# Pooling batch 0's v on VectorE from a second load, and adding the band's mask of batches 0 and 1 on TensorE

## The chip, the cores and the metric

The kernel runs on one core of one Trainium2 chip. The metric is the time of one execution on the device, in microseconds (us). A core has TensorE (PE, matrix products into PSUM), VectorE (DVE), ScalarE (ACT), GpSimd (POOL) and SyncE (SP, which issues the transfers of this kernel); each works through its own queue in order and waits for the others by semaphores. PEld is the load of a matrix into TensorE.

## What is computed

Three layers, each feeding the next, all in float32. Cut to what matters:

```python
# q, k, v: (4 batches, 8 heads, 576 rows, 64); factor 4
q_d, k_d, v_d = mean over groups of 4 rows of q, k, v          # 144 rows
out_d  = softmax(q_d @ k_d.T / 8) @ v_d                         # pooled attention
mask   = abs(i - j) < 4
out_l  = softmax(where(mask, q @ k.T / 8, -1e9)) @ v            # band attention, 7 wide
x      = repeat(out_d, 4 rows) + out_l                          # (2304, 512)
x      = (sigmoid(x @ w_gate) * (x @ w_val)) @ w_out            # layer 1, 1536 wide
h      = x @ w_in;  out = (h * sigmoid(1.702 * h)) @ w_out2     # layer 2, 2048 wide
```

## The kernel before

**Order.** The program is written as operations (`op`, line 112), each with an engine, a length in ns, the buffers that it reads and writes, and a due time. `Plan.order` (line 143) runs a list scheduler once, ahead of the launch: at each step it takes the engine that is free first and, of what is ready on it, the operation with the earliest due time; a transfer counts 230 bytes a ns and 2.2 us. The result is one fixed order for each engine. `BEGIN` (line 95) says when each engine is free of the work that stands ahead of the plan. In that plan, wherever TensorE would idle, matmuls of a constant tile `warm` into a spare PSUM bank are put in (L1420), at least one ahead of each small matmul operation until the second layer-1 product begins. `port=True` marks VectorE operations that in the plan don't overlap GpSimd's.

**Attention.** A `Job` is one batch and one pair of heads; there are four jobs to a batch, 0 to 3 being batch 0. In `pools`, GpSimd sums groups of four columns of q and k (L636, L638). `scores` computes the band in 24 tiles of 24 query rows by 30 keys into a PSUM pair of banks (L668), VectorE adds the mask while it copies the scores into `sc` (L684), takes the maximum (L694), subtracts it (L695), ScalarE takes the exponential (L697), VectorE sums, divides and transposes (L698 to L702). There is one buffer `sc`, so that a job's scores wait until the exponential of the job before has read it. The pooled scores (L710) get their softmax by L727 to L750. `down_t` transposes the pooled weights (L770, L775), `values` multiplies them by the pooled v, `vd` (L807), `band` multiplies the band's weights by v (L785), and L820 combines both. Three pairs of banks serve batch 0, one serves the other batches. Jobs 5 and later are "merged": their pooled scores share the pair of the band's scores.

**v.** `Values` holds 256 columns of v of one batch (two jobs' worth). `vt` has v in overlapping tiles of 32 rows for the band. For batches 1 to 3, `load` also brings v once more as `vg`, four rows side by side, and `pool` sums them on VectorE (L601, L603). Batch 0 has no `vg`: `pool_tiles` sums the rows of `vt` with a matrix of ones on TensorE (L590, 12 products of 256 columns, two instructions each) and ScalarE copies the result (L594). GpSimd makes the ones in 13 instructions (`make_ones`, L1367 to L1374), queued between the poolings of jobs 0 and 1.

**Layers.** A weight arrives packed in 64 bits; `convert` (L851 to L857) makes it float32 by one ScalarE and three VectorE operations, and `parts_of` (L864, L867) splits it in two parts for three products (L927, L928, L929). Four buffers receive packed weights. Layer 1 of batch 0 uses the converted weights as they come, beside attention of batch 1.

The lines that the change touches most:

```python
op("pe", 2700.0, pe, [ones, vt], [ss, vd], at)                                    # 593
op("act", act_ns(2 * VC, True), lambda: nc.scalar.copy(vd.t, ss.t[:GH, :, :VC]), [ss], [vd], at)
...
op("pool", 1500.0, make_ones, [], [ones], -4.0e3)                                 # 1377
```

Of the kernel before, what the change touches and what calls it, by code (L numbers as in the profile page):

```python
# [19 lines left out]
P = 128  # L20
# [58 lines left out]
class Plan:  # L79
# [14 lines left out]
    WARM_LEAST = 1  # L94
    BEGIN = {"pe": 0.0, "act": 2000.0, "dve": 2200.0, "pool": 3900.0, "sp": 600.0}

# [191 lines left out]
def tile_multiscale_attention_gated_ffn(  # L288
# [11 lines left out]
    D = 64  # L300
# [76 lines left out]
    for nm, n, shape in (("qt", 2, [P, S + 8]), ("kt", 2, [P, KPAD + S + 5]), ("vt", 0, [P, NG, VC]),  # L377
                         ("sc", 1, [P, 2, NG, NU]), ("pt", 2, [P, 2, NG, 32]), ("tt", 2, [P, 2, NG, 32]),
                         ("vg", 1, [GH, 2, 4, VC]), ("half", 1, [P, G, 2]),
                         ("qd", 2, [P, G]), ("kd", 2, [P, G]), ("vd", 2, [GH, 2, VC]),  # L380
                         ("pd", 2, [GH, 2, 2, G]), ("pdt", 1, [GH, 2, 2, G]), ("up", 2, [P, G]), ("ones", 1, [P, 102]),
                         ("xf", 2, [P, S])):
        aslots += ring(nm, n, shape, F32, apool)
# [5 lines left out]
    for n, x in enumerate(wslots[-8:]):  # L389
        x.under = (firsts[n // 2],)  # L390
    small = apool.tile([P, 4, 2, NG], F32, name="small", tag="small")
    smalld = apool.tile([GH, 4, 4], F32, name="smalld", tag="smalld")
# [75 lines left out]
    warm = sb.tile([P, P], BF16, name="warm", tag="warm")  # L468
    nc.vector.memset(warm, 0.0)
    for s in [*qslots, *plan.rings["qt0"][0]]:  # L470
# [36 lines left out]

    def dma(out_, in_, nbytes, reads, writes, due, after=0.0):
        op("sp", nbytes, lambda: nc.sync.dma_start(out=out_, in_=in_), reads, writes, due, after)

# [29 lines left out]
    class Values:  # L540
# [6 lines left out]
        def load(self):  # L547
# [30 lines left out]

        def pool_tiles(self):


            vt, vd = self.vt, self.vd
            at = self.job.due(0.55)
            ss = bank(self.job.banks)

            def pe():
                for g in range(NG):
                    for kh in range(2):
                        ks, o = slice(64 * kh, 64 * kh + 64), 30 - 6 * g
                        nc.tensor.matmul(ss.t[:GH, kh, :VC], ones.t[ks, o:o + GH], vt.t[ks, g],  # L590
                                         start=g == 0, stop=g == NG - 1, tile_position=(64 * kh, 0))

            op("pe", 2700.0, pe, [ones, vt], [ss, vd], at)
            op("act", act_ns(2 * VC, True), lambda: nc.scalar.copy(vd.t, ss.t[:GH, :, :VC]), [ss], [vd], at)  # L594

        def pool(self):
            if not self.b:
                return self.pool_tiles()
            vg, vd = self.vg, self.vd
            at = self.job.due(0.4)  # L600
            op("dve", dve_ns(4 * VC), lambda: nc.vector.tensor_add(  # L601
                vg.t[:, :, :2], vg.t[:, :, :2], vg.t[:, :, 2:]), [], [vg], at, port=True)
            op("dve", dve_ns(2 * VC), lambda: nc.vector.tensor_add(vd.t, vg.t[:, :, 0], vg.t[:, :, 1]),  # L603
               [vg], [vd], at, port=True)

    class Job:
# [49 lines left out]
        def scores(self):  # L656
# [15 lines left out]
            when = self.due(0.1)  # L672
            if not self.merged:
                op("pe", 1500.0, scored, [qt, kt], [ss, sc], when)
            else:
                qd, kd, nmd, smd, pd = self.qd, self.kd, self.nmd, self.smd, self.pd

                def pe():
                    scored()
                    self.pooled(ss, n)  # L680

                op("pe", 1700.0, pe, [qt, kt, qd, kd],
                   [ss, sc, nmd, (smd, 0), (smd, 1), (pd, 0), (pd, 1)], when)
            op("dve", dve_ns(2 * n), lambda: nc.vector.tensor_add(  # L684
                sc.t.rearrange("p h g c -> p h (g c)"), ss.t[:, :, :n],
                mask.rearrange("p g c -> p (g c)")[:, None, :].to_broadcast([P, 2, n])), [ss], [sc], when)
            if self.merged:
                self.pooled_softmax(ss, n, when, [sc])

# [3 lines left out]
            at = self.due(0.15)  # L693
            op("dve", dve_ns(2 * n), lambda: nc.vector.reduce_max(nm.t, sc.t, axis=AX.X), [sc], [nm], at)  # L694
            op("dve", dve_ns(2 * n), lambda: nc.vector.tensor_sub(sc.t, sc.t, spread(nm)), [nm], [sc], at, port=True)  # L695
            p = pt.t[:, :, :, :NU]
# [666 lines left out]

    ones = buf("ones")

    def make_ones():
        nc.gpsimd.memset(ones.t, 0.0)  # L1367
        for i in range(4):
            c = 30 + 36 * (i % 2)
            part = ones.t[32 * i:32 * i + 32, c:c + 6]  # L1370
            nc.gpsimd.memset(part, 1.0)
            nc.gpsimd.affine_select(out=part, in_=part, pattern=[[-4, 6]], compare_op=ALU.is_ge,
                                    fill=0.0, base=-3, channel_multiplier=1)
            nc.gpsimd.affine_select(out=part, in_=part, pattern=[[4, 6]], compare_op=ALU.is_ge,  # L1374
                                    fill=0.0, base=6, channel_multiplier=-1)
# [8 lines left out]
    for n in range(2):  # L1384
        halves[0, n].vt, halves[0, n].vd = buf("vt"), buf("vd")
    halves[0, 0].load()
    back = []
    for n in range(len(jobs) + 1):
# [9 lines left out]
        if n + 2 < len(jobs):  # L1398
            if n + 2 >= NHP:
                jobs[n + 2].load()  # L1400
            if n % 2 == 0:
                halves[divmod(n // 2 + 1, 2)].load()
# [63 lines left out]
```

## Time and profile before

| | |
|---|---|
| median of 3 runs | 923.15 us (922.99 to 925.22) |
| the profiled execution | 925.11 us |
| its span in the trace | 923.4 us |
| TensorE busy | 909.3 us, 98% |
| VectorE busy | 757.0 us, 82% |
| ScalarE busy | 508.3 us, 55% |
| GpSimd busy | 80.8 us, 9% |
| DMA moved | 113.76 MB, mean 123 GB/s |

The span is what the trace covers. All lines of the sections below come from this one execution. Busy shares are means over stages that differ: attention of batch 0 alone (to about 46 us), then layer 1 of batch 0 with attention of batch 1 beside it, and so on, so the stages have to be looked at one by one. A matmul's end is modelled in the trace and overlaps the next one's start.

### The profile page before, as it was taken

How to read it: one execution, taken by the hardware profiler on the slowest of the kernel's cores; microseconds unless marked ns; L12 is line 12 of the kernel's file. 1: busy time of each engine (PE TensorE's matmuls, PEld its weight loads, DVE VectorE, ACT ScalarE, POOL GpSimd, SP SyncE). 2: the span in 40 equal slices, each digit the busy share in tenths (PEclk: the TensorE clock that was granted, in tenths of full speed). 3: DMA queues.
4: the chain of work that ended last, by engine and by line, in shares of the span. 5: the costliest groups of instructions: out<-in, count | busy, mean ns of one | idle time of the engine just before them, and what ended most of it. 6: DMA issues, size and time to landing. Idle time of an engine off the chain costs nothing.

```text
span 923.4 us, 18997 instructions
## 1 busy us (share of the span) xinstructions
PE 909.3 (98%) x7378; PEld 761.8 (83%) x7378; DVE 757.0 (82%) x1432; ACT 508.3 (55%) x1094; POOL 80.8 (9%) x123
## 2 busy tenths in 40 slices
PE   8999999999999999999999999999999999999997
PEld 4677787788888887889999998888888888888896
DVE  4899998988878888899999898878977887765474
ACT  3756664645555555565545655545664553554463
POOL 6211201111011100010000000000301100000000
PEclk8999999999999999999999999999999999999999
DMA  9448548365375834434311651102531100152101
GB/s 287 124 155 229 188 157 244 110 183 174 114 204 185 248 108 135 159 110 141 109 49 42 222 193 46 46 24 84 190 115 69 46 35 34 40 180 78 43 4 23
DMA packets 63949, 113.76 MB, mean 123 GB/s; under 512 B 8241, under 2 KB 29563, under 8 KB 63858
## 3 DMA queue, kind: packets, MB, share of 16 engines
q1 hardware_dynamic: 63858, 112.54, 39.2%
q8 instruction: 58, 0.95, 0.5%
q14 instruction: 33, 0.27, 0.1%
HBM read 82.37 MB, written 30.15 MB: 122 GB/s over the span
## 4 chain that ended last, share of the span: by engine, by line
PE 94%; DVE 2%; POOL 1%; DMA 1%; issue 1%; ACT 1%; POOLq 0%; ACTq 0%
PE ph L927 13%; PE ph L929 13%; PE ph L928 13%; PE acc L927 8%; PE acc L928 8%; PE acc L929 8%; PE pa L927 7%; PE pa L928 7%; PE pa L929 7%; PE pa L785 2%; PE pa L668 1%; PE pa L710 1%; PE pa L770 1%; PE pa L807 1%; PE acc L1420 1%
## 5 line engine op out<-in xcount | busy, mean ns | idle before, releaser
L864 ACT CAST whi<-w 128x512 fp32r<-128x512 f32 x151 | 92.4, 613 | 77.4 <-PE ph L929 28.3
L927 PE MATMUL ph<-xhi,whi 128*128 128x512 f32 (+1 forms) x322 | 127.6, 396 | 0.0
L929 PE MATMUL ph<-xlo,whi 128*128 128x512 f32 (+1 forms) x322 | 124.4, 386 | 0.0
L928 PE MATMUL ph<-xhi,wlo 128*128 128x512 f32 (+1 forms) x322 | 124.4, 386 | 0.0
L867 DVE TENSOR_TENSOR wlo<-w,whi 128x512 fp32r<-128x512 f32 x149 | 103.9, 699 | 17.5 <-ACT whi L864 17.3
L864 ACT CAST whi<-wr 128x512 fp32r<-128x512 f32 (+1 forms) x99 | 55.7, 565 | 35.9 <-PE acc L929 16.5
L867 DVE TENSOR_TENSOR wlo<-wr,whi 128x512 fp32r<-128x512 f32 (+1 forms) x99 | 62.2, 630 | 15.6 <-ACT whi L864 14.7
L927 PE MATMUL acc<-ghi,whi 128*128 128x512 f32 (+1 forms) x192 | 73.7, 384 | 0.0
L927 PEld LDWEIGHTS ph<-xhi,whi 128*128 128x128 f32 x322 | 60.9, 189 | 14.7 <-issue 1.6
L1041 DVE TENSOR_TENSOR w<-pa,w 128x512 f32<-128x512 f32 (+1 forms) x112 | 70.2, 627 | 3.3 <-PE pa L929 2.6
L928 PE MATMUL acc<-ghi,wlo 128*128 128x512 f32 (+1 forms) x192 | 72.4, 377 | 0.4 <-DVE wlo L867 0.4
L929 PE MATMUL acc<-glo,whi 128*128 128x512 f32 (+1 forms) x192 | 72.3, 377 | 0.5 <-DVE glo L867 0.5
L929 PEld LDWEIGHTS ph<-xlo,whi 128*128 128x128 f32 x322 | 60.8, 189 | 12.5
L928 PEld LDWEIGHTS ph<-xhi,wlo 128*128 128x128 f32 x322 | 61.0, 189 | 11.3
L927 PE MATMUL pa<-w,whi 128*128 128x512 f32 (+1 forms) x168 | 61.5, 366 | 0.1
L929 PE MATMUL pa<-w,whi 128*128 128x512 f32 (+1 forms) x168 | 61.4, 366 | 0.0
L928 PE MATMUL pa<-w,wlo 128*128 128x512 f32 (+1 forms) x168 | 61.4, 366 | 0.0
L864 ACT CAST w<-w 128x512 fp32r<-128x512 f32 x51 | 31.1, 619 | 35.7 <-PE pa L929 20.4
L867 DVE TENSOR_TENSOR w<-w,w 128x512 fp32r<-128x512 f32 x48 | 34.3, 721 | 17.0 <-ACT w L864 16.8
L961 ACT ACTIVATE th<-ph 128x512 f32<-128x512 f32 (+1 forms) x44 | 24.6, 559 | 42.8 <-PE ph L929 42.8
L927 PEld LDWEIGHTS acc<-ghi,whi 128*128 128x128 f32 x192 | 36.0, 188 | 7.4 <-issue 1.7
L966 DVE SCALAR_TENSOR_TENSOR th<-th,ph 128x512 f32<-128x512 f32 (+1 forms) x44 | 27.9, 634 | 17.1 <-PE ph L929 12.2
(286 smaller groups left out, 2307.0 us busy)
## 6 DMA issues: line engine op xcount, KB each, us to landing
w<-w SPq DMA_DIRECT2D x68, 512.0 KB
w2d<-we SPq DMA_DIRECT2D x32, 256.0 KB
w<-gd SPq DMA_DIRECT2D x32, 256.0 KB
gd<-w SPq DMA_DIRECT2D x30, 256.0 KB
st<-x2d SPq DMA_DIRECT2D x52, 128.0 KB
w<-w2d SPq DMA_DIRECT2D x16, 256.0 KB
wr<-w2d SPq DMA_DIRECT2D x16, 256.0 KB
out<-ev SPq DMA_DIRECT2D x16, 256.0 KB
```

Source lines behind the costliest of these rows:

```text
L668: nc.tensor.matmul(ss.t[32 * i:32 * i + 32, h, g * NU:(g + 1) * NU], qt.t[hs, NQ * t:NQ * t + 32], kt.t[hs, NQ * t:NQ * t + NU], start=Tru ...
L710: nc.tensor.matmul(ss.t[:GH, h, c + r * G:c + (r + 1) * G], qd.t[h * D:(h + 1) * D, r * GH:(r + 1) * GH], kd.t[h * D:(h + 1) * D, :], star ...
L770: nc.tensor.transpose(ss.t[:GH, h, o:o + GH], pd.t[:, h, r, kh * GH:(kh + 1) * GH], ident.t[:GH, :GH])
L785: nc.tensor.matmul(ss.t[h * D:(h + 1) * D, s, q:q + NQ], vt.t[ks, g, v0 + h * D:v0 + (h + 1) * D], tt.t[ks, h, g, :NQ], start=True, stop=T ...
L864: op("act", act_ns(n), lambda: nc.scalar.copy(vh(), vm()), [rm], [rh], due)
L867: return lambda: on.tensor_sub(vl(), vm(), vh().bitcast(F32))
L927: nc.tensor.matmul(o, lhi, rhi, start=first, stop=False, skip_group_check=more)
L928: nc.tensor.matmul(o, llo, rhi, start=False, stop=False, skip_group_check=more)
L929: nc.tensor.matmul(o, lhi, rlo, start=False, stop=last, skip_group_check=more)
L961: op("act", act_ns(n, True), lambda h=h: nc.scalar.activation(th.t[:, :n], h.t[:, :n], AF.Tanh, scale=0.5 if layer == 1 else 1.702 / 4.0), ...
L966: op("dve", dve_ns(n), lambda: nc.vector.scalar_tensor_tensor(th.t[:, :n], th.t[:, :n], 1.0, hb[-1].t[:, :n], op0=ALU.add, op1=ALU.mult), ...
L1041: op("dve", dve_ns(N), lambda: nc.vector.tensor_add(tmp.t[:, o, :N], b.t[:, :N], tmp.t[:, i, :N]), [b, (tmp, i)], [(tmp, o)], t)
```

## The change

Half 0 of batch 0's v is loaded a second time into `vg`, half 1 into two new buffers `vg1`, which lie where layer-1 weights 10 and 11 come later. `pool` sums both halves on VectorE; for half 1 the two row blocks are loaded and summed apart. `pool_tiles`, the ones and their products go. For batches 0 and 1 the mask is kept in bf16, and TensorE adds it: a product of the identity (bf16, now the content of `warm`) and the mask opens each accumulation, the scores are added to it, and VectorE's maximum and subtraction read the scores from PSUM. Batches 2 and 3 keep the add on VectorE. The identity is made first on GpSimd, in bf16, and VectorE copies it to float32.

```diff
-    BEGIN = {"pe": 0.0, "act": 2000.0, "dve": 2200.0, "pool": 3900.0, "sp": 600.0}
+    BEGIN = {"pe": 0.0, "act": 2000.0, "dve": 4400.0, "pool": 4300.0, "sp": 600.0}
...
+    seconds = [Slot(x.rearrange("p a b -> p (a b)").bitcast(F32).rearrange("p (r d) -> p r d", r=4)[:GH])
+               for x in top[2:4]]
+    plan.ring("vg1", seconds)
+    for n, x in enumerate(wslots[20:24]):
+        x.under = (seconds[n // 2],)
...
-    nc.vector.memset(warm, 0.0)
+    make_identity(nc, warm)
...
-    mask = sb.tile([P, NG, NU], F32, name="mask", tag="mask")
+    mask = sb.tile([P, 2, NG, NU], BF16, name="mask", tag="mask")[:, 0]
...
+    maskb = mask.rearrange("p g c -> p (g c)")
-    op("pool", 650.0, lambda: make_identity(nc, ident.t), [], [ident], -10.0e3)
+    nc.vector.tensor_copy(ident.t, warm)
...
+                if hp:
+                    self.vg = [buf("vg1") for _ in range(2)]
+                else:
+                    self.vg = buf("vg")
+                for kh in range(2):
+                    x, t = (self.vg[kh], self.vg[kh].t) if hp else ((self.vg, kh), self.vg.t[:, kh])
+                    dma(t, v[b, kh * 4 * GH:(kh + 1) * 4 * GH, c].rearrange("(g r) d -> g r d", r=4),
+                        GH * 4 * VC * 4, [], [x], -16.5e3 if hp else -19.1e3, 13.0e3 if hp else 6.0e3)
...
-        def pool_tiles(self):
...
+            if isinstance(vg, list):
+                for kh, x in enumerate(vg):
+                    op("dve", dve_ns(2 * VC), lambda x=x: nc.vector.tensor_add(x.t[:, :2], x.t[:, :2], x.t[:, 2:]),
+                       [], [x], at, port=True)
+                    op("dve", dve_ns(VC), lambda kh=kh, x=x: nc.vector.tensor_add(vd.t[:, kh], x.t[:, 0], x.t[:, 1]),
+                       [x], [(vd, kh)], at, port=True)
+                return
...
+            masked = self.b < 2
             def scored():
+                for h in range(2 if masked else 0):
+                    nc.tensor.matmul(ss.t[:, h, :n], warm, maskb, start=True, stop=False, skip_group_check=True)
...
-                                         start=True, stop=True, tile_position=(h * D, 32 * i))
+                                         start=not masked, stop=True, tile_position=(h * D, 32 * i),
+                                         skip_group_check=masked)
...
-            op("dve", dve_ns(2 * n), lambda: nc.vector.tensor_add(
+            x = ss if masked else sc
+            if not masked:
+                op("dve", dve_ns(2 * n), lambda: nc.vector.tensor_add(
...
+            def scores_of():
+                return ss.t[:, :, :n].rearrange("p h (g c) -> p h g c", c=NU) if masked else sc.t
+            op("dve", dve_ns(2 * n), lambda: nc.vector.reduce_max(nm.t, scores_of(), axis=AX.X), [x], [nm], at)
+            op("dve", dve_ns(2 * n), lambda: nc.vector.tensor_sub(sc.t, scores_of(), spread(nm)),
+               [nm, x] if masked else [nm], [sc], at, port=not masked)
...
-    op("pool", 1500.0, make_ones, [], [ones], -4.0e3)
...
-    halves[0, 0].load()
+    for n in range(2):
+        halves[0, n].load()
```

## Rows read from the trace of the kernel before

**Rows 1.** The page, part 4: the chain that ended last, by engine.
```profile
PE 94%; DVE 2%; POOL 1%; DMA 1%; issue 1%; ACT 1%; POOLq 0%; ACTq 0%
```
**Rows 2.** Windows (us): busy us (instructions) of PE, PEld, DVE, ACT, POOL; clock; DMA share; GB/s.
```profile
12.00:46.00 34.00, 31.94 (x836) 21.80 (x837) 24.48 (x51) 21.65 (x65) 10.73 (x16) 0.90 0.63 198
46.00:135.00 89.00, 88.28 (x1069) 69.79 (x1068) 86.54 (x158) 56.03 (x130) 12.46 (x13) 1.00 0.62 183
```
**Rows 3.** Timeline of GpSimd: start, length, line, output and input; [idle before and releaser].
```profile
6.93 0.18 POOL L1367 MEMSET ones<- 128x102 f32 x1
...
10.39 0.67 POOL L636 TENSOR_TENSOR half<-qt 128x288 f32<-128x288 f32 x1
...
15.14 0.67 POOL L636 TENSOR_TENSOR half<-w 128x288 f32<-128x288 f32 x1 [2.17 <-DMA w<-qT]
```
**Rows 4.** Timeline of TensorE, 7 to 25 us; neighbours of one kind are merged (x).
```profile
7.94 1.69 PE L1420 MATMUL acc<-warm 128*128 128x512 bf16 x7
13.03 1.24 PE L710 MATMUL pa<-kd,qd 64*72 64x144 f32 x8 [3.41 <-POOL kd L638]
...
14.74 1.22 PE L668 MATMUL acc<-kt,qt 64*32 64x30 f32 x96
...
16.43 4.17 PE L590 MATMUL acc<-vt,ones 64*72 64x256 f32 x24
...
21.57 2.81 PE L590 MATMUL pa<-vt,ones 64*72 64x256 f32 x24
```
**Rows 5.** Window 12 to 19 us, columns as in Rows 2.
```profile
12.00:19.00 7.00, 5.97 (x118) 3.65 (x120) 3.97 (x9) 3.08 (x13) 4.36 (x8) 0.53 1.04 356
```
**Rows 6.** Timeline of ScalarE: the copy of the pooled v, the first weight's conversion.
```profile
20.68 0.58 ACT L594 COPY vd<-acc 72x512 f32<-72x512 f32 x1 [3.79 <-PE acc L590]
...
24.91 0.66 ACT L851 ACTIVATE wr<-w 128x512 f32<-128x512 f32 x1
```
**Rows 7.** Timeline of VectorE: three operations that waited.
```profile
22.53 0.54 DVE L698 TENSOR_REDUCE small<-pt 128x12 f32<-128x372 f32 x1 [4.36 <-ACT pt L697]
...
28.17 0.76 DVE L820 TENSOR_TENSOR xf<-acc,up 128x576 f32<-128x576 f32 x1 [0.68 <-PE acc L785]
...
34.31 0.76 DVE L820 TENSOR_TENSOR xf<-pa,up 128x576 f32<-128x576 f32 x1 [0.69 <-PE pa L785]
```
**Rows 8.** Windows of 7.1 to 46 us, columns as in Rows 2.
```profile
7.10:25.60 18.50, 15.09 (x231) 8.87 (x232) 9.50 (x20) 9.20 (x32) 9.56 (x25) 0.82 0.88 276
25.60:46.00 20.40, 19.37 (x623) 13.98 (x622) 18.64 (x38) 14.59 (x43) 5.09 (x6) 1.00 0.50 136
```
**Rows 9.** Lines L601, L603, L684, L695: count, ns shortest/median/longest, first and last start.
```profile
L601 DVE TENSOR_TENSOR vg<-vg x6: 1209/1214/1216, 63.2 to 306.9; 72x1024 f32<-72x1024 f32 x6
L603 DVE TENSOR_TENSOR vd<-vg x6: 677/680/680, 64.9 to 310.6; 72x512 f32<-72x512 f32 x6
L684 DVE TENSOR_TENSOR sc<-acc,mask x3: 495/524/531, 16.0 to 36.3; 128x360 f32<-128x360 f32 x3
L695 DVE TENSOR_TENSOR sc<-sc,small x16: 518/533/716, 8.8 to 360.0; 128x360 f32<-128x360 f32 x16
```
**Rows 10.** Timeline of SP: one load of vg for batch 1 being issued.
```profile
29.53 0.82 SPq L509 DMA_DIRECT2D vg<-v  x1
```
**Rows 11.** Windows of 1 us, columns as in Rows 2: the DMA share and GB/s are last.
```profile
8.00:9.00 1.00, 1.00 (x7) 0.44 (x6) 1.00 (x3) 0.05 (x1) 0.82 (x4) 1.00 1.09 221
...
21.00:22.00 1.00, 1.00 (x12) 0.65 (x12) 0.00 (x0) 0.80 (x3) 0.00 (x0) 1.00 1.03 393
...
24.00:25.00 1.00, 1.00 (x29) 0.46 (x28) 0.51 (x1) 0.57 (x2) 0.00 (x0) 1.00 0.00 0
...
34.00:35.00 1.00, 1.00 (x68) 0.74 (x67) 0.69 (x2) 0.27 (x2) 0.00 (x0) 1.00 0.84 180
```
**Rows 12.** Timeline of TensorE at 140 us, in layer 1 of batch 0.
```profile
140.20 0.89 PE L785 MATMUL pa<-tt,vt 30*64 30x24 f32 x48 [1.09 <-DVE tt L702]
```
**Rows 13.** Window right behind it, columns as in Rows 2.
```profile
142.00:144.00 2.00, 2.00 (x6) 1.56 (x6) 2.00 (x4) 0.65 (x2) 0.00 (x0) 0.52 0.91 339
```

More of the change, by code (lines that the diff above doesn't have):

```diff
@@ L380, in tile_multiscale_attention_gated_ffn @@
                          ("qd", 2, [P, G]), ("kd", 2, [P, G]), ("vd", 2, [GH, 2, VC]),
-                         ("pd", 2, [GH, 2, 2, G]), ("pdt", 1, [GH, 2, 2, G]), ("up", 2, [P, G]), ("ones", 1, [P, 102]),
+                         ("pd", 2, [GH, 2, 2, G]), ("pdt", 1, [GH, 2, 2, G]), ("up", 2, [P, G]), ("pad", 1, [P, 102]),
                          ("xf", 2, [P, S])):
@@ L506, in pool_ns, with dma @@
         return 140.0 + 2.12 * n
-    def dma(out_, in_, nbytes, reads, writes, due, after=0.0):
-        op("sp", nbytes, lambda: nc.sync.dma_start(out=out_, in_=in_), reads, writes, due, after)
+    def dma(out_, in_, nmaskeds, reads, writes, due, after=0.0):
+        op("sp", nmaskeds, lambda: nc.sync.dma_start(out=out_, in_=in_), reads, writes, due, after)
     QUANTUM = 3 * 227.0
@@ L577, in load @@
                 d, after)
-        def pool_tiles(self):
[L582 to L594, printed above, removed]
         def pool(self):
-            if not self.b:
-                return self.pool_tiles()
             vg, vd = self.vg, self.vd
             at = self.job.due(0.4)
+            if isinstance(vg, list):
[5 more added lines that the diff above has]
+                return
             op("dve", dve_ns(4 * VC), lambda: nc.vector.tensor_add(
@@ L669, in scored @@
                                          qt.t[hs, NQ * t:NQ * t + 32], kt.t[hs, NQ * t:NQ * t + NU],
-                                         start=True, stop=True, tile_position=(h * D, 32 * i))
+                                         start=not masked, stop=True, tile_position=(h * D, 32 * i),
+                                         skip_group_check=masked)
             when = self.due(0.1)
             if not self.merged:
-                op("pe", 1500.0, scored, [qt, kt], [ss, sc], when)
+                op("pe", 1500.0 + 200.0 * masked, scored, [qt, kt], [ss, sc], when)
             else:
@@ L680, in pe @@
                     self.pooled(ss, n)
-                op("pe", 1700.0, pe, [qt, kt, qd, kd],
+                op("pe", 1700.0 + 200.0 * masked, pe, [qt, kt, qd, kd],
                    [ss, sc, nmd, (smd, 0), (smd, 1), (pd, 0), (pd, 1)], when)
-            op("dve", dve_ns(2 * n), lambda: nc.vector.tensor_add(
-                sc.t.rearrange("p h g c -> p h (g c)"), ss.t[:, :, :n],
-                mask.rearrange("p g c -> p (g c)")[:, None, :].to_broadcast([P, 2, n])), [ss], [sc], when)
+            x = ss if masked else sc
+            if not masked:
+                op("dve", dve_ns(2 * n), lambda: nc.vector.tensor_add(
+                    sc.t.rearrange("p h g c -> p h (g c)"), ss.t[:, :, :n],
+                    mask.rearrange("p g c -> p (g c)")[:, None, :].to_broadcast([P, 2, n])), [ss], [sc], when)
             if self.merged:
-                self.pooled_softmax(ss, n, when, [sc])
+                self.pooled_softmax(ss, n, when, [x])
             def spread(x):
@@ L693, in scores @@
             at = self.due(0.15)
-            op("dve", dve_ns(2 * n), lambda: nc.vector.reduce_max(nm.t, sc.t, axis=AX.X), [sc], [nm], at)
-            op("dve", dve_ns(2 * n), lambda: nc.vector.tensor_sub(sc.t, sc.t, spread(nm)), [nm], [sc], at, port=True)
+            def scores_of():
[3 more added lines that the diff above has]
+               [nm, x] if masked else [nm], [sc], at, port=not masked)
             p = pt.t[:, :, :, :NU]
@@ L1362, in tile_multiscale_attention_gated_ffn @@
     seven = [0]
[L1364 to L1375, printed above, removed]
-    op("pool", 1500.0, make_ones, [], [ones], -4.0e3)
     jobs = [Job(b, hp) for b in range(B) for hp in range(NHP)]
@@ L1400, in tile_multiscale_attention_gated_ffn @@
                 jobs[n + 2].load()
-            if n % 2 == 0:
+            if n % 2 == 0 and n:
                 halves[divmod(n // 2 + 1, 2)].load()
```

## The prediction

> **What bounds the kernel now.** I read the page's chain first: TensorE carries 94% of it [rows 1]. That is a mean over stages, so I read the stages next [rows 2]. From 46 to 135 us TensorE is busy 88.28 of 89 us, but VectorE is busy 86.54 of the same 89, since it turns the layer-1 weights into fp32 and splits them there. Both engines are full, and neither can gain alone. From 12 to 46 us, where attention of batch 0 runs, VectorE is busy only 24.48 of 34 us. All that the change touches in batch 0 lies there, so I followed who waits for whom.
>
> Three stalls hang together. (1) GpSimd builds the matrix of ones from 6.93 us on and comes to job 1's pooling of q and k only at 10.39, 3.4 us later but for gaps [rows 3]; TensorE sits idle for 3.41 us until that pooling ends at 13.0 [rows 4]. Job 1's scores, whose data are there, are queued behind the waiting matmul and come at 14.74. [...] (3) The pooling of v by the ones takes 4.17 us there and 2.81 us once the clock is back, 7.0 in all [rows 4]. ScalarE has the copy of its result next in its queue and waits 3.79 us for it; VectorE waits 4.36 us for job 1's exponential, which is behind that copy [rows 6, 7]. So in 7.1 to 25.6 us VectorE is busy 9.50 of 18.50 us: 9.0 us idle. From 25.6 to 46 it is idle 1.76 us [rows 8].
>
> The profiled execution took 925.1 us (span 923.4 and 1.7 around it); the median is 923.15, 2.0 less. I sum against 925.1 and take 2.0 off at the end.
>
> **The change part by part.** *TensorE.* The 7.0 us of pooling go. The ones go from GpSimd, so job 1's q and k can be pooled right after job 0's: end near 7.0 + 2.6 = 9.6 us instead of 13.0 (2.6 is 13.03 less 10.39, the same four operations before). Job 1's scores, behind it in the queue, move as far, to some 11.3. If the idle is gone the clock need not fall; of the 3.4 us of other work at 13.0 to 16.4 about half, 1.5 us, comes back. Together TensorE could stand 3.4 + 7.0 + 1.5 = 12 us earlier. Added are two bf16 matmuls of 180 columns per job in 8 jobs. No row has them. Seven bf16 matmuls of 512 columns take 1.69 us, 0.24 each [rows 4]; scaled by columns 0.085, unscaled 0.24, so 16 cost 1.4 to 3.9 us. They only add work, so no gain is possible. I take 1.4, since columns are what such a matmul streams; half of it lies in batch 0 beside slack, 0.7 in batch 1 on a full TensorE.
>
> *VectorE.* The mask's add, 0.525 us, goes from 8 jobs: 2.1 us in batch 0, 2.1 in batch 1 [rows 9]. Added in batch 0: for half 0 the two adds of batches 1 to 3, 1.214 and 0.68 us; for half 1 two pairs of half that length. By the line through those two rows, 1.04 ns an element, the pair costs 0.68 and 0.41, twice 1.09. Sum 4.07. Net in batch 0: +2.0 us; in batch 1: -2.1.
> The maximum and the subtraction now read PSUM. The add, which reads PSUM, takes 0.524 us and the subtraction, from SBUF, 0.533 [rows 9], so I price that at nothing; ends: -0.02 and +0.02 us each. [...]
> The scores' PSUM pair is held through the maximum and the subtraction, about 1.06 us longer. Batch 0 has three pairs and loses the two holders of the pooling; in batch 1 the merged jobs hold their pair for the exponentials anyway. Nothing, with that cover; without it 1 us a job.
>
> *ScalarE* loses both copies and, what counts, the wait ahead of the first [rows 6].
>
> *DMA and SP.* Four loads of 0.295 MB, in runs of 1 KB, are issued: two ahead of the q and k of jobs 2 and 3, two between those and the first weights. Each issue holds SP about 0.82 us [rows 10], 3.3 in all. The engines are full until about 22 us [rows 11], so the bytes cost more than the issue. No row has this load alone in the same place: v's tiles go at 221 GB/s early on, and the 1 KB runs of batch 1 near 180; q, k and weights at 393 [rows 11]. Hence 1.18 MB take 3.0 to 6.6 us; I take 5.3 (221), the row in the same traffic. The first q of job 2, awaited until 15.1 us [rows 3], lands near 17.8 (two loads, 2.7 us, now stand ahead of it). The weights land about 5.3 us later. Their cover: DMA stands still at 24 to 25 us [rows 11] while the first converted weight is only touched at 24.91 [rows 6]. So the first conversion need not start later than before, but it cannot start earlier either.
> [...]
> In VectorE's queue the adds can wait for these loads, with job 1's softmax behind them; that is in the idle below.
>
> *Small moves.* The identity is now made first on GpSimd, so the warming matmuls begin later by its time, and the scores of job 0 with them; the missing add repays it. VectorE's copy of the identity ends long before the first scores. Nothing.
>
> **The sum.** TensorE gains 12 us but can use only what VectorE feeds it. VectorE has 9.0 us idle before 25.6. I keep 4.0 of it: the wait for the first scores, the exponential of job 0, and the later data of jobs 2 and 3; this is an estimate, with ends 2 (the first two alone) and 7 (the loads bind). Lead at 25.6 us: 9.0 - 4.0 - 2.0 = 3.0. Of the idle after that, two waits of 0.68 and 0.69 us for TensorE's last band product go [rows 7]: 4.4. Batch 1's masks give 2.1 more by 135 us and cost TensorE 0.7; this counts only where VectorE is late, as at 140 us, where TensorE waits 1.09 us for it [rows 12]. I count 0.6 and forecast 5.0 us. Afterwards TensorE is the bound and nothing gives it back. 925.1 - 5.0 = 920.1, less 2.0: **918.1 us**. With the ends of the kept idle, 7 and 0 for batch 1, 2 and all of its 2.1: 1.4 to 8.5 us, 921.7 to 914.6.
>
> **The rivals.** *TensorE is the bound after all.* If weights are early enough, nearly all 12 us arrive, less 0.7: 925.1 - 11.3 - 2.0, about 912. For: TensorE's 94% of the chain. Against: VectorE's 97% in the same stage.
> *The new loads eat it.* At 180 GB/s weights come 6.6 us late, VectorE runs out of attention work before they land, and the kept idle is 7 or more. The lead is then 0 at 25.6 and the rest 0 to 1.4: 921.7 to 923.2, call it 922.5. For: DMA is full until 22 us. Against: the engines stood still at 24 us with weights at hand. That the new order keeps conversions where they were gives the same time.
> *Slower: TensorE starved in the first layer.* With less to do in front, TensorE stands ahead of VectorE and waits for weights from 46 to 140 us. The place at 140 us shows the price of one such wait: 1.09 us, and then 0.52 of full clock for 2 us, which loses 1.0 more [rows 12, 13]: 2.1 a time. A lead of 1.4 is used up by one; three more cost 6.3, with 0.7 for the masks: 923.15 - 1.4 + 6.3 + 0.7 = 928.8. It decides from the second wait on if the lead is small, the fourth if it is 5. For: VectorE has 2.5 us of slack in 89. Against: the change takes 2.1 us from VectorE just there.
>
> **How the numbers follow.** Forecast 0.48 (915 to 920.3 as its own range), TensorE as the bound 0.16, loads eat it 0.23, slower 0.13. The range reaches to the second and third case, 910 to 926; below it and above it lie some 0.18. About 0.3%, 2.8 us, is what a measurement of this kernel can tell from no change: faster 0.64, same 0.23, slower 0.13.
>
> **What would show it.** After: job 1's scores near 11 us; no granted clock of 0.5 over some 7 us around 12 to 19; ScalarE without a wait of 3.8 us; VectorE at least 13 of 18.5 us busy before 25.6; the DMA engines full until about 28 us; jobs 2 and 3 done several us earlier, and TensorE's long back-to-back stretch with them. I am wrong if the first conversion comes later than 27 us, if VectorE waits over 2 us for a second load, or if the clock falls again in 46 to 140 us.

## The result, and the profile after

The changed kernel took 933.03 us (median of 4, 931.51 to 938.16) against 923.68 us for the kernel before beside it: ratio 1.0113, 95% interval 1.0089 to 1.0137. It is 1.1% slower. The profiled execution took 932.86 us, span 931.0, 7.6 us longer than before's.

The page's chain by engine, which answers [rows 1]:

```profile
PE 93%; DVE 3%; issue 2%; ACT 1%; POOL 1%; POOLq 0%; DVEq 0%; ACTq 0%
```

"issue" went from 1% to 2%. Windows of the kernel after, columns as in [rows 2]; the first two answer [rows 2], the next two [rows 8], and the last two are where the clock was low:

```profile
12.00:46.00 34.00, 25.87 (x610) 16.36 (x613) 20.41 (x41) 15.80 (x54) 10.89 (x14) 0.75 0.76 205
46.00:135.00 89.00, 88.10 (x1037) 69.06 (x1031) 79.86 (x148) 53.12 (x120) 10.76 (x13) 0.92 0.61 174
7.10:25.60 18.50, 13.62 (x355) 8.44 (x355) 11.37 (x25) 8.68 (x32) 7.80 (x12) 0.91 1.07 269
25.60:46.00 20.40, 15.34 (x366) 9.96 (x368) 12.87 (x25) 9.58 (x33) 5.17 (x6) 0.67 0.55 153
28.00:41.50 13.50, 9.69 (x217) 6.34 (x217) 6.75 (x15) 4.87 (x18) 1.83 (x3) 0.50 0.58 145
48.80:62.40 13.60, 13.60 (x174) 10.05 (x173) 9.23 (x16) 5.01 (x9) 1.74 (x2) 0.51 0.48 153
```

Batch 0's attention is not limited by VectorE any more, nor by anything else that computes: from 25.6 to 46 us VectorE is busy 12.87 us (18.64 before), TensorE 15.34 (19.37 before), and the clock is 0.67 instead of 1.00. From 46 to 135 us VectorE has gained 6.7 us of slack that nobody uses, because TensorE runs some 14 us of that stretch, from 48.6 us on, at the lower clock, 0.51. What TensorE waits for stands in its timeline (start, length, line, output and input, count; idle before it and its releaser):

```profile
9.49 0.71 PE L724 MATMUL pa<-kd,qd 64*72 64x144 f32 x8 [1.36 <-POOL kd L640]
...
10.61 0.95 PE L674 MATMUL acc<-kt,qt 64*32 64x30 f32 x88
15.07 0.33 PE L674 MATMUL acc<-kt,qt 64*32 64x30 f32 x8 [3.51 <-issue]
...
27.94 1.37 PE L799 MATMUL pa<-tt,vt 30*64 30x24 f32 x48 [1.24 <-ACT xhi L845]
...
31.23 0.94 PE L674 MATMUL acc<-w,w 64*32 64x30 f32 x69
35.99 0.45 PE L674 MATMUL acc<-w,w 64*32 64x30 f32 x27 [3.81 <-issue]
...
47.40 0.18 PE L799 MATMUL acc<-tt,vt 30*64 30x24 f32 x1 [0.83 <-issue]
```

Job 1 is pooled and its scores begin at 10.61 us, as forecast. Then TensorE stops with 88 of the 96 products done, in the middle of one operation, and goes on 3.51 us later. "issue" means that the profile shows nothing that it waited for. The same at 31.9 us, 69 products into an operation, for 3.81 us. In the first stop every engine stands still, while the transfers run on (the window 12 to 15 us):

```profile
12.00:15.00 3.00, 0.00 (x0) 0.00 (x0) 0.00 (x0) 0.00 (x0) 0.00 (x0) 0.91 1.09 227
```

What it waits for is one of those transfers. The profile's DMA view lists, per queue, packets, MB and the time that they took as a share of 16 engines. Queue q8 of the kernel after in the windows 12.2 to 12.3, 25.5 to 25.6 and 33.2 to 33.3 us:

```profile
q8 instruction: 1, 0.02, 82.5%
...
q8 instruction: 1, 0.02, 68.9%
...
q8 instruction: 1, 0.02, 79.6%
```

Queue q8 brings instructions, 57 packets of 16,384 bytes in the whole run for 7351 matmuls: one for 129. That they are TensorE's shows in their number: 58 for the 7378 matmuls of before, 55 for the 7031 of e10, while a second instruction queue, q14, has 33 packets on every page. Each of these three windows has the start of one packet; the share, of 16 engines times 0.1 us, is a packet of 1.3, 1.1 and 1.3 us. By their starts and lengths in the trace they land at 13.5, 26.7 and 34.6 us, and TensorE goes on at 15.07, 27.94 and 35.99, 1.2 to 1.5 us later.

Counting matmuls from the start of the timeline shows the rule of it. The table has, for the first 66 us of each kernel of this study, every wait of TensorE of at least 0.3 us that ends at one of the counts 222, 349, 476, 604, 731, 858 (within two, since some records are missing). The steps are 127 or 128. Each row is read from one execution.

| kernel | 222 | 349 | 476 | 604 | 731 | 858 |
|---|---|---|---|---|---|---|
| before | | | | 0.73 | | |
| after | 3.51 | | 1.24 | 3.81 | | 0.83 |
| e1 without the second loads | 4.23 | | | | | 1.79 |
| e2 masks only | 4.81 | | | | 1.40 | |
| e3 pooling only | 1.48 | 5.92 | | | | 0.58 |
| e4 before, with the loads | | | | | | |
| e5 lone warming doubled | 3.05 | | 1.85 | 1.67 | | 1.86 |
| e6 ones made again | 0.47 | | 1.32 | 3.74 | | 0.56 |
| e7 before, lone warming out | | | 0.52 | | | |
| e8 half 1 late | 4.86 | | 1.85 | 0.58 | | 0.38 |
| e9 job 0 with 4 products | | 1.02 | | | | |
| e10 batch 0 with 8 products a job | | | | 0.34 | | |
| e11 first warming out | | 0.58 | | 1.90 | | 1.25 |
| e12 late, warming out | | 3.92 | | 1.50 | | |
| f1 fill at 28 us | 3.71 | | 0.76 | 3.12 | | 1.99 |
| f2 half 1 late, fill | 4.52 | | 1.87 | | | 0.89 |
| f3 batch 0 few, fill | | | | | | |
| f4 before, fill | 0.38 | | | 1.07 | 1.96 | |

In these 66 us every wait over 0.35 us that the trace calls "issue" ends at such a count. Three that it puts down to ScalarE do too (the 1.24 us at 27.94, e8's 1.85 and e11's 1.25). In all 42 entries of the table, these three among them, TensorE goes on 1.2 to 1.9 us after a packet of q8 has landed, so these three were probably waits for instructions as well. So in these runs TensorE's instructions come in pieces of about 127 matmuls, and where a piece had not landed TensorE stopped, whatever operation stood there: up to 5.92 us (e3).

That fits batch 0's loss. The removed pooling was 48 matmuls that took 7.0 us [rows 4], so one piece lasted long: TensorE took 10.8 us from count 222 to 349 in before, 6.3 in after. Without the pooling the pieces hold band products of 30 columns, 96 in 1.0 us, and are used up faster than they come. In the kernel after the packets start in the windows 12, 16, 25, 33, 37 and 44 us: up to 9 us apart. The packets for the counts 476 and 604 start only 4.2 and 5.4 us after TensorE has passed the count before.

**Where the 7.6 us of span are.** From windows of 1 us over the first 150: TensorE idle 12.2 us (7.3 before), busy time lost to the lower level, a granted clock of 0.50 (busy times 1 minus clock), 13.2 us (4.8 before): 13.3 more. The removed pooling at full clock is 5.6 (twice 2.81 [rows 4]). That leaves 7.7. After 150 us neither sum differs by over 0.5 us. The agreement is closer than the method: the masks add about 2 us that this leaves out, and some lower-level time fell on warming matmuls that nobody waits for. Mean clock tells the same: 0.993 before, 0.983 after, and 0.010 of 912.7 us busy is 9.1.

### The profile page after: what moved, and what is told of

Its sections match the earlier page's. It is cut to its first block, busy times and chain, and to the rows that moved or that the text cites. A ratio compares the mean times of both kernels' runs of the same rounds, so it can differ in the third digit from the quotient of the medians.

```text
span 931.0 us, 18927 instructions
## 1 busy us (share of the span) xinstructions
PE 912.7 (98%) x7351; PEld 764.9 (82%) x7351; DVE 755.6 (81%) x1430; ACT 505.8 (54%) x1092; POOL 82.7 (9%) x110
## 4 chain that ended last, share of the span: by engine, by line
PE 93%; DVE 3%; issue 2%; ACT 1%; POOL 1%; POOLq 0%; DVEq 0%; ACTq 0%
PE ph L941 13%; PE ph L943 13%; PE ph L942 13%; PE acc L941 8%; PE acc L942 8%; PE acc L943 8%; PE pa L941 7%; PE pa L943 7%; PE pa L942 7%; PE pa L799 2%; PE pa L674 1%; PE pa L821 1%; PE pa L784 1%; PE pa L724 1%; PE acc L799 1%
## 5 line engine op out<-in xcount | busy, mean ns | idle before, releaser
L980 DVE SCALAR_TENSOR_TENSOR th<-th,ph 128x512 f32<-128x512 f32 (+1 forms) x44 | 28.0, 635 | 18.2 <-PE ph L943 13.3
```

The lines of the kernel that those rows point to most:

```text
L980: op("dve", dve_ns(n), lambda: nc.vector.scalar_tensor_tensor(th.t[:, :n], th.t[:, :n], 1.0, hb[-1].t[:, :n], op0=ALU.add, op1=ALU.mult), ...
```

## The experiments

The letters in the expectations: A, the added traffic delays TensorE's instructions; B, the small matmuls use instructions faster than they come, with any traffic; C, it is the masks or the new order; D, the removed products of 256 columns kept the clock up; E, the ones' removal was no gain, since TensorE is out of instructions there anyway; W and N, falls of the clock follow waits, or don't.

### The parts of the change

**e1_no_loads.** The changed kernel with the four second loads left out; the sums read the tiles of the band.

```diff
-                    dma(t, v[b, kh * 4 * GH:(kh + 1) * 4 * GH, c]...., [], [x], ...)
+                    op("sp", GH * 4 * VC * 4, lambda: None, [], [x], ...)
-    nc.vector.tensor_add(x.t[:, :2], x.t[:, :2], x.t[:, 2:])
+    nc.vector.tensor_add(x.t[:, :2], self.vt.t[:GH, :2], self.vt.t[:GH, 2:4])
```

> The changed kernel with the four second loads of v left out; the sums read batch 0's tiles instead, so the pooled v of batch 0 is not the mean over four rows. Every engine's order is that of the changed kernel. Theory A (TensorE waits for its own instructions, 3.5 us at 11.6 us and 3.8 us at 32 us, because their fetches share the DMA engines with the added traffic): both waits named issue fall under 1 us each, the clock falls less, and the time is 916 to 923 us. Theory B (the instructions of the small matmuls are simply used up faster than they can be fetched, whatever the traffic): the waits stay above 2 us each and the time stays at 929 to 933 us. Theory C (the masks and the new order cost it): issue waits may go, the time stays above 929 us.

926.42 us (10 executions, 920.10 to 934.27), ratio 1.001 (0.9988 to 1.0031). 6.6 of the 9.4 us go with the loads, 7.3 if the longest execution is left out. The time lies between the forecasts of A and B. TensorE's waits in its timeline (its profiled execution was the longest of the ten, so its lengths are to be read with care):

```profile
15.79 0.26 PE L678 MATMUL acc<-kt,qt 64*32 64x30 f32 x8 [4.23 <-issue]
45.77 0.18 PE L803 MATMUL acc<-tt,vt 30*64 30x24 f32 x1 [1.79 <-issue]
```

The stops at 476 and 604 are gone; those at 222 and 858 stay. The packets now start in the windows 19, 23 and 28 us where after has 16, 25 and 33. Those for 476 and 604 start 0.9 us after TensorE passed the count before and 0.4 us ahead of that, where in after it was 4.2 and 5.4 us after: without the loads the packets come sooner, and the stops go. So A holds for these two stops. The first doesn't come from the second loads; in e1 the packets of q1, which moves the data, take 95 to 114% of the 16 engines' time in each us from 11 to 15, with loads that both kernels have, and whether these cause it was not tried.

The clock shows something else (windows of e1, columns as in [rows 2]):

```profile
16.00:26.30 10.30, 10.30 (x245) 6.40 (x237) 7.67 (x16) 6.34 (x21) 5.46 (x8) 0.83 0.85 323
26.30:40.00 13.70, 13.70 (x240) 8.46 (x237) 10.95 (x21) 6.47 (x23) 4.42 (x5) 0.50 0.30 87
```

From 16 to 26.3 us TensorE of this execution has no idle time at all, and yet the clock is 0.50 for the 13.7 us behind. So a fall of the clock came without a wait just ahead of it.

**e2_masks_only**, **e3_pool_only**. The change's masks without its pooling, and the reverse.

```diff
 e2: pool_tiles, make_ones and their products as before; no second loads
 e3:
-            masked = self.b < 2
+            masked = False
```

> Only the masks of batches 0 and 1 move to TensorE; v of batch 0 is pooled by the ones as before, and nothing is loaded twice. Theories A and B: no wait named issue above 1.5 us, time 920 to 925 us. Theory C: 928 us or more.

> Only the pooling moves to VectorE, with its second loads; VectorE adds all masks as before. Theories A and B: one or two waits named issue above 2 us in the first 40 us, time 928 to 934 us. Theory C: 921 to 925 us.

925.85 us, ratio 1.0019 (1.0003 to 1.0035), and 937.93 us, ratio 1.0135 (1.0098 to 1.0173). The masks alone cost about 2 us, and the pooling alone at least as much as both together (its interval and that of 1.0113 overlap), so the masks are not the main cause, and C falls. But A and B had forecast no stop over 1.5 us for e2, and it stops 4.81 us at 222, with the ones and without the second loads. This costs little against before, which stands 3.41 us for GpSimd shortly ahead of that count. Their times are missed too, by 0.85 us in e2 and by 3.9 in e3. In e3 TensorE stops 5.92 us at 349:

```profile
15.58 0.33 PE L674 MATMUL acc<-kt,qt 64*32 64x30 f32 x8 [1.48 <-issue]
27.91 1.49 PE L799 MATMUL acc<-tt,vt 30*64 30x24 f32 x48 [5.92 <-issue]
```

**e4_before_loads.** The kernel before, with the four loads added, read by nobody.

```diff
+                for kh in range(0 if b else 2):
+                    nc.sync.dma_start(out=plan.rings["vg"][0][0].t[:, kh], in_=again(0, kh))
...
```

> The kernel before with the four second loads of v added in the same places of SP's queue, and nobody reading them; the other engines' orders are those of before. Theory A: TensorE's waits named issue grow from 0.7 to over 2 us and the time is 926 to 931 us. Theory B and C: TensorE's stream is unchanged, so the waits stay under 1.5 us and the time is 922 to 926 us, apart from later weights.

928.15 us, ratio 1.004 (1.0024 to 1.0056): 3.7 us. The loads cost 3.7 us on the kernel before and 6.6 us on the changed one. With the long pooling products in place TensorE never stopped for instructions; it waited 3.9 us for GpSimd and 1.5 for ScalarE, and the clock was low from 28 to 41 us (48 band products took 1.49 us at 27.71, 0.89 at 44.96). So A's time came true (926 to 931) by luck: its mechanism, stops of over 2 us, did not. So the loads have a price beside the stops, presumably through data that come later, and how their 6.6 us in the changed kernel divide between the two is not shown.

### What stands at the stops

**e6_ones_back.** The changed kernel with the ones made on GpSimd as before, for nobody.

```diff
+            def second():
+                nc.gpsimd.tensor_add(dst.t, half.t[:, :, 0], half.t[:, :, 1])
+                if (self.b, self.hp) == (0, 0) and dst is self.kd:
+                    make_ones()
```

> The changed kernel with GpSimd building the matrix of ones again after job 0's pooling, for nobody; the orders are else those of the changed kernel. Theory E (the 3.4 us before the ones' removal were no gain, because TensorE runs out of fetched instructions at 11.6 us until 15.1 whatever GpSimd does): the wait named issue there shrinks to under 1.5 us, a wait for GpSimd takes its place, and the time is 931 to 935 us, as of the changed kernel. Rival (GpSimd's 3.4 us were gained): 936 us or more.

932.34 us, ratio 1.008 (1.0054 to 1.0106): no slower than after. Its timeline:

```profile
12.42 0.71 PE L728 MATMUL pa<-kd,qd 64*72 64x144 f32 x8 [2.85 <-POOL kd L641]
15.03 0.33 PE L678 MATMUL acc<-kt,qt 64*32 64x30 f32 x8 [0.47 <-issue]
28.00 1.49 PE L803 MATMUL pa<-tt,vt 30*64 30x24 f32 x48 [1.32 <-issue]
36.11 0.45 PE L678 MATMUL acc<-w,w 64*32 64x30 f32 x27 [3.74 <-issue]
```

The last 8 scores of job 1 come at 15.03, in after at 15.07. The wait for GpSimd only stood in front of the wait for instructions. That is E: the 3.41 us of [rows 4], the first term of my sum, were not to be had. In before, too, the packet for count 222 lands only at 13.8 us; TensorE passed that count at 15.6, so that without the 3.41 us it would have been there at 12.2, ahead of its instructions.

**e8_half1_late.** Half 1's loads moved behind the first two weights.

```diff
-                        GH * 4 * VC * 4, [], [x], -16.5e3 if hp else -19.1e3, 13.0e3 if hp else 6.0e3)
+                        GH * 4 * VC * 4, [], [x], -11.5e3 if hp else -19.1e3, 18.2e3 if hp else 6.0e3)
```

> The changed kernel with the two second loads of half 1 behind the first two weights in SP's queue instead of ahead of them. Theory A (the added traffic's place is what costs): 927 to 930 us. Theories D and E (clock, and instructions at 11.6 us): 931 to 935 us.

930.88 us (925.23 to 936.95), ratio 1.007 (1.0039 to 1.01). The stop at 604 falls to 0.58 us, that at 476 stays. Some 2 us come back by the medians, but the interval overlaps that of after (1.0089 to 1.0137), and the time lies in the gap between the forecasts.

**e9_job0_few**, **e10_batch0_few.** Most band products left out, which takes matmuls out of the stream.

```diff
-                    for h in range(2):
+                    for h in range(0 if (self.b, self.hp) == (0, 0) and t >= 2 else 2):   # e9
+                    for h in range(0 if self.b == 0 and t >= 4 else 2):                   # e10
```

> The changed kernel with 44 of the 48 band products of job 0 left out (its scores are then the mask alone there): 176 instructions and 0.9 us less on TensorE, ahead of the place at 11.6 us where it waited 3.5 us. Theory E (TensorE stands there because it has used up the instructions that are fetched, 16 of them short of the end of job 1's scores): that wait is gone or under 1 us and job 1's scores end near 11 us; the time is 925 to 930 us, 3 us or more under the changed kernel. Rival (the wait has another cause, say the data of job 1): the wait stays at its place with 3 us or more, and the time is 931 to 934 us.

> The changed kernel with 40 of the 48 band products left out in all four jobs of batch 0: 640 instructions and 3.3 us less on TensorE. Theory E: no wait named issue above 1 us in the first 75 us, the time at half clock falls from 31 to under 15 us, and the time is 914 to 922 us. Rival: waits and clock stay, 928 to 931 us.

930.06 us, ratio 1.0061 (1.004 to 1.0081), and 926.54 us, ratio 1.0032 (1.0016 to 1.0048). As E expects, job 1's scores run through in both, and e10 has no stop over 0.35 us. e9's time lies just above E's range. But e10's should have been 914 to 922, and its time at the lower level in the first 75 us is 27.3 us, not under 15. The row of its scores of job 2, and the window behind it:

```profile
18.46 0.44 PE L674 MATMUL pa<-w,w 64*32 64x30 f32 x16 [1.74 <-DMA w<-kT]
```
```profile
20.00:37.00 17.00, 16.96 (x224) 10.68 (x221) 12.81 (x25) 9.00 (x30) 7.32 (x11) 0.53 0.94 237
```

Without the stops TensorE is there early, waits for the k of job 2 (behind the first two of the second loads in SP's queue; job 2's q came to GpSimd at 18.45 us in after, at 15.14 in [rows 3]), and then is busy 16.96 of 17 us at a clock of 0.53. So the stops are not the whole cause: the lower clock is a loss of its own.

### What the clock does

**e5_lone_twice**, **e7_before_no_lone.** The warming matmuls that stand singly between small operations: doubled in the changed kernel, left out of the kernel before.

```diff
+            for _ in range(2 if at in lone else 1):   # e5; e7: 0 if at in lone
+                o.fn()
```

> The changed kernel with every warming matmul of 512 columns that stands alone between two others of TensorE issued twice, some 22 more of 0.23 us at full clock, 5 us of useless work in all; the orders are else those of the changed kernel. Theory D (the removed products of 256 columns kept TensorE active, and without them its clock falls at 28 and at 48 us for some 14 us each): the time spent at half clock falls from about 31 to under 15 us and the time is 926 to 931 us, less than the changed kernel's 933. Rival (TensorE just has its list to work off, the clock falls for its waits): 935 to 938 us.

> The kernel before without the some 22 warming matmuls of 512 columns that stand alone between two others of TensorE; they take 0.23 to 0.32 us each there, 5 to 7 us of its chain. The orders are else those of before. Theory D: the clock falls for more than 15 us in the first 75, and the time is 923 us or more in spite of less work. Rival: 917 to 920 us.

936.29 us, ratio 1.0121, time at the lower level 37.6 us instead of 30.7; and 923.03 us, ratio 0.9989 (0.9971 to 1.0007), 13.7 us instead of 6.8. Twice the wide products among the small ones did not keep the clock up, and e5's time is the rival's: D, in that form, falls there. e7 comes nearer to D: its time is within D's 923 or more and not in the rival's 917 to 920, and its 13.7 us at the lower level are short of D's 15.

**e11_first_one**, **e12_late_none.** Eleven of the first twelve warming matmuls left out; and e8 with those and the single ones left out.

```diff
+            for _ in range(1 if at in lone else 0 if 0 < at < lead else 1):   # e11; e12: 0 if at in lone
+                o.fn()
```

> The changed kernel without 11 of the 12 warming matmuls of 512 columns at the very start, 22 instructions less before the place at 11.6 us; nothing else differs, and the output is whole. Theory E: job 1's scores are done before TensorE runs out of instructions, so VectorE has them near 12 us instead of 15.5; 928 to 932 us. Rival (the early matmuls are needed for the clock): the clock is at half level before 10 us, 933 us or more.

> The changed kernel with three edits: half 1's loads behind the first two weights, 11 of the first 12 warming matmuls out, and the lone ones out as well. Theories A and E (fewer instructions to fetch, less traffic where they are fetched): 922 to 928 us, near the kernel before. Rival: 930 us or more.

934.37 us, ratio 1.0117 (1.0094 to 1.014), and 933.14 us (921.79 to 938.20), ratio 1.0061 (1.0015 to 1.0107). In both the time is the rival's. In e11 job 1's scores do run through, as E says, and VectorE has them at 12.7 us, but TensorE ran more slowly up to there. Its scores of jobs 0 and 1:

```profile
4.86 1.22 PE L674 MATMUL pa<-kt,qt 64*32 64x30 f32 x96
11.48 1.21 PE L674 MATMUL acc<-kt,qt 64*32 64x30 f32 x96
```

96 products take 1.02 us at full clock and 1.22 at the lower level ([rows 4], under the clock of [rows 5]). By that e11 works at the lower level until about 15 us, as does e12 (1.21 us for each), though the clock column doesn't show it, since its records start only near 15 us in both. That is the rival of e11: the early matmuls are needed for the clock. So these two say little on how fast the pieces come.

**f1 to f4.** Warming matmuls put into one wait: after at 27 us (six more), e8 at 29 us (eight), e10 at 17 us (seven), and the kernel before in its 3.41 us wait (fourteen).

```diff
+            for _ in range({44: 7}.get(at, 1)):   # f1; f2 {44: 9}, f3 {34: 8}, f4 {21: 15}
+                o.fn()
```

> The changed kernel with six more warming matmuls of 512 columns where TensorE waited 1.24 us at 26.7 us for ScalarE, just ahead of the fall of the clock at 28 us. Theory W (a wait of TensorE is followed by the fall): the wait is filled, the clock stays up at 28 to 41 us, half-clock time 31 falls to 17 us or less, and the time to 924 to 929 us. Rival N (the clock falls because the work from 20 to 48 us is small matmuls, wait or no wait): half-clock time stays at 27 us or more, 931 to 935 us.

> The kernel with half 1's second loads behind the first weights, with eight more warming matmuls where TensorE waited 1.85 us at 28.7 us. W: the fall at 31 us does not come, half-clock time 17 falls to 7 to 10 us, 923 to 928 us. N: half-clock time stays at 17 us or more, 929 to 934 us.

> The changed kernel with 40 of 48 band products of the four jobs of batch 0 left out, which had no wait for instructions over 0.4 us and yet half-clock time of 27 us, with seven more warming matmuls where TensorE waited 1.74 us at 16.7 us for the q of job 2. W: no fall at 20 us, half-clock time 14 us or less, 918 to 922 us. N: half-clock time 20 us or more, 925 to 928 us.

> The kernel before with fourteen more warming matmuls in the 3.41 us that TensorE waits for GpSimd at 9.6 to 13.0 us. W: the clock does not fall at 12 to 19 us, half-clock time 7 falls to 0 to 3 us, and 3 us of the time go: 920 to 922 us. N: the half-clock time stays, or another wait puts it elsewhere: 923.5 to 925.5 us.

| | us | ratio | lower level, us |
|---|---|---|---|
| f1 | 933.71 | 1.0111 (1.0091 to 1.0131) | 23.9 (after 30.7) |
| f2 | 932.03 | 1.0087 (1.0056 to 1.0119) | 23.9 (e8 17.1) |
| f3 | 926.39 | 1.0026 (1.0008 to 1.0044) | 34.1 (e10 27.3) |
| f4 | 924.66 | 1.0009 (0.9994 to 1.0023) | 6.8 (before 6.8) |

N's forecast came true in f2, f3 and f4, and f1's time is N's too. W's came true in none as a whole, but two falls went. In f4 the wait was filled but for 0.25 us. In f1 it was not: the stop at 476 came ahead of the six matmuls, and was shorter than in after (0.76 us, not 1.24):

```profile
13.35 0.71 PE L710 MATMUL pa<-kd,qd 64*72 64x144 f32 x8 [0.25 <-POOL kd L638]
```
```profile
28.11 1.46 PE L1420 MATMUL ph<-warm 128*128 128x512 bf16 x6 [0.76 <-issue]
```

Windows of f4, to be read beside [rows 5] (0.53), and of f1, beside 28 to 41.5 us of after:

```profile
12.00:19.00 7.00, 6.37 (x137) 3.67 (x135) 4.52 (x10) 3.09 (x14) 4.01 (x7) 1.00 1.04 352
34.00:41.00 7.00, 5.04 (x27) 2.73 (x17) 4.08 (x10) 2.91 (x13) 2.32 (x3) 0.51 0.32 82
```
```profile
28.00:34.00 6.00, 4.06 (x128) 2.55 (x127) 3.42 (x5) 2.52 (x11) 0.99 (x1) 1.00 0.88 213
36.00:42.00 6.00, 6.00 (x66) 3.32 (x66) 5.00 (x11) 3.38 (x11) 2.56 (x4) 0.50 0.27 79
```

In f4 the clock stays at 1.00 from 12 to 19 us, in f1 from 28 to 34. f4 is as W says. But TensorE then comes sooner to the next piece (f4 stops 1.07 and 1.96 us at 604 and 731, f1 3.12 at 604), and the clock falls again, from 34.0 us in f4, 1.8 us behind the first of its stops, and from 35.5 in f1, right behind its stop. In f2, too, the stop at 476 comes ahead of the filling matmuls, and in f3 the later transfer makes the wait 2.79 us; nothing was filled. In f2 the clock fell at 30.6 us all the same, but was back at 34.0, behind the eight wide matmuls (L821's 8 products take 0.71 us at 34.34); in e8, without them, it was low from 31.2 to 41.5 (the same 8 take 1.23 at 31.50). So W's rule is seen in one kernel, f4, and e1 has a fall without a wait; W's times were wrong, and the kernel before has no 3 us to gain from its wait either.

The four kernels also show that it is a count. One operation, cut by the stop at 604, in after with 6 more matmuls ahead of it (f1), and with 11 fewer (e11); and another in before, and with 14 more (f4):

```profile
31.44 0.74 PE L674 MATMUL acc<-w,w 64*32 64x30 f32 x63
35.29 0.45 PE L674 MATMUL acc<-w,w 64*32 64x30 f32 x33 [3.12 <-issue]
```
```profile
32.86 1.08 PE L674 MATMUL acc<-w,w 64*32 64x30 f32 x80
35.84 0.36 PE L674 MATMUL acc<-w,w 64*32 64x30 f32 x16 [1.90 <-issue]
```
```profile
32.37 0.76 PE L785 MATMUL pa<-tt,vt 30*64 30x24 f32 x36
33.86 0.41 PE L785 MATMUL pa<-tt,vt 30*64 30x24 f32 x12 [0.73 <-issue]
```
```profile
30.63 0.54 PE L785 MATMUL pa<-tt,vt 30*64 30x24 f32 x22
32.23 0.59 PE L785 MATMUL pa<-tt,vt 30*64 30x24 f32 x26 [1.07 <-issue]
```

After stops behind 69 products of that operation; f1 behind 63, which is 69 less 6; e11 behind 80, which is 69 and 11. Before stops behind 36, f4 behind 22, which is 36 less 14.

No kernel here beat the kernel before; e1, e7 and f4 are level with it, within their intervals.

## Why the prediction was wrong

**The step that failed** is the first of the sum: "Together TensorE could stand 3.4 + 7.0 + 1.5 = 12 us earlier". It took a TensorE that waits for no other engine for one that runs. Of the 12 us: the 3.4 had a second wait right behind it (e6: 15.03 against 15.07). The 7.0 were long products on few instructions, and so the cover under which a piece came; in their place are stops of 1.24 and 3.81 us. The 1.5, for a clock that need not fall, is shown by no run: with the clock at 1.00 from 12 to 19 us f4 took 924.66 us, level with before, and in after the clock was 0.50 from 28 to 41.5 us and 0.51 from 48.8 to 62.4. How much earlier TensorE really stood shows at the first and last of the four groups of band products of jobs 0 and 1; the first line is before's, the others after's:

```profile
24.64 0.89 PE L785 MATMUL acc<-tt,vt 30*64 30x24 f32 x48
```
```profile
21.86 0.89 PE L799 MATMUL acc<-tt,vt 30*64 30x24 f32 x48
...
36.91 1.49 PE L799 MATMUL pa<-tt,vt 30*64 30x24 f32 x48
```

The first group comes 2.8 us earlier, not 12; the last, at 32.37 in before, comes 4.5 us later. The trace of before had the sign: the 0.73 us at 33.86, an "issue" wait in the middle of an operation, with no engine to blame. I did not ask what it was.

**"If the idle is gone the clock need not fall."** The idle moved to the stops, and the time at the lower level in the first 75 us went from 6.8 to 30.7 us. The rule held where the wait was really filled (f4), but it is not the whole of it: in e1 the clock fell with no idle time for 10 us ahead.

**VectorE as the bound.** It was to be at least 13 us busy in 7.1 to 25.6 us; it was 11.37, with 7.1 idle, the far end of the 2 to 7 that I gave. The rival by which the loads eat it has that end. But 7 idle was not the end of it, because I had summed only up to a point from which TensorE would be the bound and lose nothing.

**The loads.** The size was about right. GpSimd got the q of job 2 at 18.45 us (17.8 said), the first conversion began at 30.70, 5.8 us later than [rows 6] (5.3 said):

```profile
18.45 0.66 POOL L638 TENSOR_TENSOR half<-w 128x288 f32<-128x288 f32 x1 [9.02 <-DMA w<-qT]
```
```profile
30.70 0.66 ACT L865 ACTIVATE wr<-w 128x512 f32<-128x512 f32 x1
```

The cover was wrong: I set the 5.3 us against the standstill of the engines at 24 to 25 us and let the conversion start as before; over 27 us was named as a sign of being wrong. And the loads had a second price that no term held: TensorE's own instructions come as transfers too, and two of their packets started 4.2 and 5.4 us after TensorE had passed the count before, but 0.9 us after and 0.4 ahead without the loads (e1).

**The small terms.** Masks: 1.4 us for 16 products, scaled by columns; [rows 4] has 0.117 us for 256 columns (24 in 2.81) and 0.24 for 512. But a pair takes 0.24 to 0.25 us from start to start at full clock, 0.12 for 180 columns where the scaling gave 0.085, so 8 pairs take 2.0. Maximum and subtraction from PSUM: 0.524 and 0.532 us against 0.514 and 0.533 from SBUF, nothing, as priced from [rows 9]. Half 1's sums: 1.04 us for the first pair as priced (1.09), 2.17 for the second. Masks at 140 us: that 1.09 us wait is gone.

**The rivals.** The slower one had the sign, which was luck, and a clock fall behind each wait, but the wrong place and engine: from 46 to 135 us TensorE is busy 88.10 of 89 us, and no wait there is over 0.9 us. 933 lies above its 928.8 and above my range.

**Left open.** What makes the clock fall: it fell in e1 with no wait just ahead and near 45 to 49 us behind waits of 0.3 us in e10 and 0.8 in after, but not behind 0.73 us in before or 0.76 in f1. What made the fall at 20 us in e10 last 17 us with TensorE busy throughout. In the rows the clock came back during or right behind a run of wide products: from 39.5 to 44 us in after, f1 and f3 (six and seven warming matmuls), at 62 with layer-1 products back to back, and in f2 behind eight (in after it was 1.00 from 41.8 to 48.6 us and from 62.3 to 80). That such runs bring it back was not tried by itself. How the loads' price divides between instructions that come late and data that come late is not settled, nor what holds up the first stop's packet.

## What to carry to other kernels

Before counting on an engine that will "stand earlier", count its instructions, not only its microseconds: look for "issue" waits inside an operation, and ask whether the work that goes away is what gives the next instructions time to come. An idle stretch is worth only what it has ahead of the next wait; putting the old wait back (e6), or filling it (f4), tells cheaply what that is. A transfer added for its data can delay the instruction stream as well: here two packets came later by 3 to 6 us against TensorE's progress (e1).

## What the runs showed of the hardware

- TensorE's instructions arrived while the kernel ran, as transfers: 57 packets of 16,384 bytes for 7351 matmuls in after, with the stops 127 or 128 matmuls apart or a multiple of that. The longest, 5.92 us, ended at 27.91 in e3, where the packets that move data took 96 to 114% of the 16 DMA engines' time in each us from 22 to 28. In all 42 stops of the table it went on 1.2 to 1.9 us after a packet had landed.
- In after the granted clock was 0.50 for 13.5 us behind the stop of 1.24 us that ended at 27.94. That the stop made it fall is not shown, and a busy TensorE had the lower level too: in e10 it was busy 16.96 of 17 us at a clock of 0.53, in e1 13.70 of 13.70 at 0.50.
- Executions of one kernel differed by over 1%, the longest with a lower mean clock than the shortest: e8 took 925.23 us at 0.992 and 936.95 at 0.981.
